# First attention pair of a clustered attention: its first head loaded to both halves of the partitions, its second head's clusters later

## The chip, the cores and the metric

One Trainium2 chip, one of its cores. The metric is the device time of one execution in microseconds. The core has TensorE (matmuls, PE in the rows), VectorE (DVE), ScalarE (ACT), GpSimd (POOL) and SyncE (SP, whose queue issues most transfers). Each engine runs its own list of instructions in order and waits on the others by semaphores.

## What is computed

Queries and keys of 16 pairs of batch and head are assigned to one of 16 clusters each, by the largest product with the normalized centroids; attention is taken inside a cluster only. Two MLPs follow.

```python
q_assign = np.argmax(np.einsum('bhsd,hcd->bhsc', q_n, c_n), axis=-1)
k_assign = np.argmax(np.einsum('bhsd,hcd->bhsc', k_n, c_n), axis=-1)
mask = q_assign[:, :, :, None] == k_assign[:, :, None, :]
scores = np.where(mask, scale * np.matmul(q, k.transpose(0, 1, 3, 2)), -1e9)
attn = softmax(scores)          # B=2, H=8, S=768, D=64
x = attn @ v                    # then x -> silu MLP -> gated MLP, 1536 tokens
```

All of it is float32 in quality: an operand is split in a rounded high part and a low part, and both go through the matmul.

## The kernel before

Heads go in pairs, p = 0 to 7, one head on partitions 0 to 63 (`L`) and one on 64 to 127 (`U`). A pair has 12 tiles of 128 queries, (p, j, i) with j the head and i = 0 to 5; "tile 0 to 5" below are those of the first head of pair 0. For each tile `scores` (L463) makes four matmuls into a PSUM buffer `s` of which there are two: two from `qa`, `ka`, in which the high part of a head stands on one half of the partitions and the low part of the query on the other, and two from `qm`, `km` (called `q` and `k` in the rows), which hold the high query, the low key and 16 rows each for the cluster masks. VectorE takes the negative maximum `nm`, ScalarE the exponential `e`, TensorE transposes `e` into `u` and `t` (two and four transposes), which VectorE and ScalarE copy into `ring` (called `ph`), and `values` (L511) multiplies with `vv`. A tile's `s` can be written again when the exponential two tiles before is done.

Clusters: `product_of_clusters` (L152) multiplies queries and keys with the centroids `cc` into `pm`, `scaled` (L276) brings them into `sums` (tile `sim`) on ScalarE, `similarities` (L165) transposes them into `ps`, and `ranked` (L170) finds on VectorE the maximum `mx`, the equal ones `eq`, their ranks `wq` and the first of them `mw`; two operations then write the choice `oh`. `choice_rows` transposes `oh` into `pt`, and `query_rows` and `key_rows` write the mask rows.

Pair 0 is written by hand ahead of the loop (L186 to L370). TensorE first runs `warm(n)`, products of zeros. The loads `qq`, `kk` bring both heads, one on each half; ScalarE makes the high parts `qh`, `kh` and VectorE the low part `ql`; nine transfers from buffer to buffer on SP's queue put them into `qa`, `ka` and `qm` of both heads. One `product_of_clusters` serves both heads. The first head is ranked from `ps` (`first_choice(0, ...)`), the second later from `sums` (`first_choice(1, ...)` in `first_masks`, L341). `zeros` clears operands and `oh` on GpSimd; `mine` on GpSimd copies `mw`, and only behind it the second head's clearing and its low key `late` are issued.

What sets the order: up to the end of `first` (L618) the instructions of TensorE, VectorE, ScalarE and SP stand as written; behind it only TensorE's do, and a scheduler places those of the other engines. In the loop `one_tile` (L648) runs the score of the tile two ahead, pieces of the next pair's preparation (`PIECES`, L643; the second head's masks are among the first of them), and the transposes of the tile.

## Time and profile before

| what | us |
|---|---|
| median of 3 runs | 773.4 |
| lowest, highest | 773.12, 774.94 |
| the profiled execution | 772.8 |
| its span, first to last instruction | 771.0 |
| TensorE busy in it | 761.3 (99%) |
| VectorE, ScalarE, GpSimd busy | 621.0, 403.5, 391.8 |

Rows give times from the start of the span. Busy times of matmuls overlap, and their ends are modelled; what matters is when one starts, what it waited for, and who waits for it.

### The profile page before, as it was taken

How to read it: one execution, taken by the hardware profiler on the slowest of the kernel's cores; microseconds unless marked ns; L12 is line 12 of the kernel's file. 1: busy time of each engine (PE TensorE's matmuls, PEld its weight loads, DVE VectorE, ACT ScalarE, POOL GpSimd, SP SyncE). 2: the span in 40 equal slices, each digit the busy share in tenths (PEclk: the TensorE clock that was granted, in tenths of full speed). 3: DMA queues.
4: the chain of work that ended last, by engine and by line, in shares of the span. 5: the costliest groups of instructions: out<-in, count | busy, mean ns of one | idle time of the engine just before them, and what ended most of it. 6: DMA issues, size and time to landing. Idle time of an engine off the chain costs nothing.

```text
span 771.0 us, 11463 instructions
## 1 busy us (share of the span) xinstructions
PE 761.3 (99%) x4314; PEld 652.6 (85%) x4314; DVE 621.0 (81%) x787; ACT 403.5 (52%) x691; POOL 391.8 (51%) x345
## 2 busy tenths in 40 slices
...
GB/s 222 159 203 194 114 146 195 122 123 201 32 76 79 57 83 83 55 110 82 88 78 82 54 55 58 88 75 56 34 76 55 82 83 55 55 82 55 1 0 164
DMA packets 25488, 71.61 MB, mean 93 GB/s; under 512 B 4484, under 2 KB 4952, under 8 KB 25432
## 3 DMA queue, kind: packets, MB, share of 16 engines
...
q8 instruction: 34, 0.56, 0.3%
...
HBM read 48.01 MB, written 3.19 MB: 66 GB/s over the span
## 4 chain that ended last, share of the span: by engine, by line
PE 92%; DVE 3%; ACT 2%; DMA 1%; issue 1%; POOL 0%; SPq 0%; ACTq 0%
PE z L1018 13%; PE s L468 8%; PE v L515 8%; PE t L507 5%; PE y L959 4%; PE h_0w L843 4%; PE h_0x L843 4%; PE g_0w L843 3%; PE g_0x L843 3%; PE v_0w L843 3%; PE v_0x L843 3%; PE u L496 3%; PE r L909 2%; PE q L909 2%; PE y_00None L959 2%; PE y_20None L959 2%
## 5 line engine op out<-in xcount | busy, mean ns | idle before, releaser
L476 DVE TENSOR_REDUCE nm<-s 128x1 f32<-128x768 f32 x96 | 91.5, 954 | 11.2 <-PE s L468 10.1
L481 ACT ACTIVATE e<-s,nm 128x768 f32<-128x768 f32 x96 | 86.5, 901 | 26.4 <-DVE nm L476 25.9
L1018 PE MATMUL z<-wu,ghb 128*128 128x512 f32 (+1 forms) x292 | 89.5, 388 | 0.0
L515 PE MATMUL v<-ph,vv 128*64 128x384 f32 x384 | 69.0, 494 | 0.2 <-DVE xf L527 0.2
L1018 PEld LDWEIGHTS z<-wu,ghb 128*128 128x128 f32 x292 | 54.2, 188 | 11.6 <-ACT ghb L64 0.5
L468 PE MATMUL s<-ka,qa 128*128 128x384 f32 x192 | 57.7, 381 | 2.0 <-ACT e L481 1.7
L507 PE MATMUL t<-ident,e 128*128 128x128 f32 x384 | 58.5, 275 | 0.8 <-ACT ph L64 0.3
L1018 PE MATMUL z<-wu,glb 128*128 128x512 f32 (+1 forms) x146 | 56.9, 390 | 0.0
L515 PEld LDWEIGHTS v<-ph,vv 128*64 128x64 f32 x384 | 24.7, 136 | 32.9 <-issue 29.0
L64 ACT ACTIVATE ph<-t 128x512 f32<-128x512 f32 x68 | 40.8, 600 | 21.4 <-PE t L507 20.5
L468 PE MATMUL s<-k,q 128*128 128x384 f32 x192 | 49.7, 339 | 0.0
L939 DVE TENSOR_TENSOR acc<-z,acc 128x1024 f32<-128x1024 f32 (+2 forms) x32 | 36.7, 1154 | 13.9 <-PE z L1018 13.2
L507 PEld LDWEIGHTS t<-ident,e 128*128 128x128 f32 x384 | 44.0, 140 | 4.2 <-DVE ph L67 3.2
L67 DVE COPY ph<-u 128x512 f32<-128x512 f32 x48 | 32.8, 683 | 16.3 <-PE u L496 16.3
L546 POOL TENSOR_TENSOR acc<-xf,rb 128x768 f32<-128x768 f32 x7 | 12.8, 1835 | 58.9 <-DVE nm L476 25.5
L496 PEld LDWEIGHTS u<-ident,e 128*128 128x128 f32 x192 | 23.3, 141 | 22.3 <-issue 18.6
L738 POOL TENSOR_TENSOR wo<-co,wo 128x512 fp32r<-128x512 f32 x16 | 22.0, 1383 | 35.5 <-ACT wo L64 35.5
L496 PE MATMUL u<-ident,e 128*128 128x128 f32 x192 | 38.6, 282 | 0.5 <-ACT e L481 0.5
L468 PEld LDWEIGHTS s<-k,q 128*128 128x128 f32 x192 | 34.5, 188 | 0.5 <-ACT k L338 0.3
L468 PEld LDWEIGHTS s<-ka,qa 128*128 128x128 f32 x192 | 28.9, 190 | 5.3 <-ACT e L481 3.4
L1018 PEld LDWEIGHTS z<-wu,glb 128*128 128x128 f32 x146 | 27.4, 188 | 7.0 <-DVE glb L899 1.4
L959 PE MATMUL y<-gha,wo 128*128 128x384 f32 x128 | 32.8, 334 | 0.0
...
## 6 DMA issues: line engine op xcount, KB each, us to landing
...
```

Source lines behind the costliest of these rows:

```text
L64: return nc.scalar.activation(o, i, AF.Copy)
L67: return nc.vector.tensor_copy(o, i)
L468: nc.tensor.matmul(s[:, g, 0:HS], lhsT=a[:, j, i * P : (i + 1) * P], rhs=c[:, j, g * HS : (g + 1) * HS], start=n == 0, stop=n == 1,)
L476: maxima.append(nc.vector.tensor_reduce(nm, s[:, :, 0:HS], axis=AX.XY, op=ALU.max, negate=True))
L481: x = nc.scalar.activation(e, s[:, :, 0:HS], AF.Exp, bias=nm, scale=1.0, accum_out=tots[p][:, n : n + 1])
L496: nc.tensor.transpose(both[:, kt - 4, i % 2, :], e[:, kt * P : (kt + 1) * P], ident)
L507: nc.tensor.transpose(t[:, kt, :], e[:, kt * P : (kt + 1) * P], ident)
L515: m = nc.tensor.matmul(o[(L, U)[kt % 2]], lhsT=vv[:, j, kt, :], rhs=ring[:, kt, g * G : (g + 1) * G], start=n < 2, stop=n >= NT - 2,)
L843: nc.tensor.matmul(o[:, b, 0:HS], lhsT=w[a][s][:, k, :], rhs=right[b, q][t][:, k, :], start=start and k == 0 and n == 0, stop=k == KQ - 1 ...
L939: added.append(nc.vector.tensor_tensor(z, o, z, op=ALU.add))
L959: nc.tensor.matmul(o[:, d, 0:width], lhsT=s[:, d, k, :], rhs=t[:, c], start=k == 0 and m == 0, stop=k == 1 and m == 2,)
L1018: nc.tensor.matmul(o[:, a, c], lhsT=s[:, q * P : (q + 1) * P], rhs=r[:, c], start=k == 0 and m == 0, stop=k == 1 and m == 2, skip_group_ch ...
```

## The change

In pair 0 the first head's queries and keys come from a new input `heads0` ([64, 2, 768]), loaded twice, onto rows 0 to 63 and onto rows 64 to 127 of the first two rows of `ring`, which is otherwise used only from the first transposed tile on. Its operands are cast from there straight into `ka`, `qa`, `qm`, `km`, and the low query is subtracted in place, so no transfer between buffers is left for it. `qq` and `kk` are loaded for the second head alone (rows 64 to 127); GpSimd splits it, and five transfers place it. The centroids arrive as one tile `ct` on all partitions and are copied by VectorE into the two places in `cc`.

The clusters' products become two calls: the first head's from rows 0 to 63 of the staged operands, at the old place; the second head's from rows 64 to 127 of `qq`, `kk`, behind the transposes of the first head's choice. Its scaling, transposes (`ps0_1`, behind tile 1's scores) and the cast into `sums` follow later too. `mine` goes; the second head's clearing stands ahead. The warming products are 7, 1, 4, 5 instead of 10, 1, 8, 5. Which engine copies which half of the first head's key rows is exchanged.

```diff
-WARM = (10, 1, 8, 5)
+WARM = (7, 1, 4, 5)
...
-        def product_of_clusters(pm, p, q, k):
+        def product_of_clusters(pm, p, q, k, rows=slice(0, P)):
...
-                        lhsT=cc[:, p % HP].rearrange("p j c -> p (j c)"),
-                        rhs=t.rearrange("p (i h c) -> p h i c", h=2, c=P)[:, h],
+                        lhsT=cc[rows, p % HP].rearrange("p j c -> p (j c)"),
+                        rhs=t[rows].rearrange("p (i h c) -> p h i c", h=2, c=P)[:, h],
...
-        for j, r in enumerate((L, U)):
-            act_dma(cc[r, :, j], cenT[j])
+        ct = cp.tile([P, HP, C], F32, tag="ct", name="ct")
+        act_dma(ct, cenT)
+        ring = wk.tile([P, NT, S], F32, tag="ph", name="ph", bufs=1)
+        staged = ring[:, 0], ring[:, 1]
+        for r in (L, U):
+            dma(ring[r, 0:2], heads0)
...
-        dma(qq, qT[0, 0])
-        dma(kk, kT[0, 0])
+        for t, a in zip((qq, kk), (qT, kT)):
+            dma(t[U], a[0, 0][U])
...
             zeros(0, 0)
+            zeros(0, 1)
...
+        for j, r in enumerate((L, U)):
+            nc.vector.tensor_copy(cc[r, :, j], ct[r])
...
-        nc.scalar.activation(qh, qq, AF.Copy, scale=scale)
-        nc.vector.scalar_tensor_tensor(ql, qq, scale, qh, op0=ALU.mult, op1=ALU.subtract)
-        cast(nc.scalar, kh, kk)
-        nc.vector.tensor_tensor(km[L, 0], kk[L], kh[L], op=ALU.subtract)
-
-        for j, (r, o) in enumerate(((L, U), (U, L))):
-            dma(qa[r, j].bitcast(F32), qh[r].bitcast(F32))
-            dma(ka[L, j].bitcast(F32), kh[r].bitcast(F32))
-            dma(ka[U, j].bitcast(F32), kh[r].bitcast(F32))
-            dma(qa[o, j].bitcast(F32), ql[r].bitcast(F32))
-            if j:
-                dma(qm[r, j].bitcast(F32), qh[r].bitcast(F32))
-        dma(vv, v[0, 0])
-
+        sq0, sk0 = staged
+        cast(nc.scalar, ka[L, 0], sk0[L])
+        nc.gpsimd.tensor_scalar(qm[L, 0], sq0[L], scale, 1.0, op0=ALU.mult, op1=ALU.mult)
         pm = ps_s.tile([P, 512], F32, tag="s", name="pm0")
-        product_of_clusters(pm, 0, qq, kk)
+        product_of_clusters(pm, 0, sq0, sk0, L)
         warm(WARM[1])
+        nc.vector.tensor_tensor(km[L, 0], sk0[L], ka[L, 0].bitcast(F32), op=ALU.subtract)
...
         scaled(0, sums, pm[:, 0:HS])
-        nc.scalar.activation(qm[L, 0], qq[L], AF.Copy, scale=scale)
...
         similarities(ps, sums)
+        nc.scalar.activation(qa[:, 0], sq0, AF.Copy, scale=scale)
+        cast(nc.scalar, ka[U, 0], sk0[U])
+        cast(nc.gpsimd, kh[U], kk[U])
+        nc.gpsimd.tensor_scalar(qh[U], qq[U], scale, 1.0, op0=ALU.mult, op1=ALU.mult)
         warm(WARM[2])
+        ex = sm.tile([P, 1], F32, tag="ex", name="ex", bufs=1)
+        nc.scalar.activation(ex, unit[:, 0:1], AF.Exp)
...
         for _ in first_choice(0, ps[:, 0:HS]):
             pass
-        cast(nc.scalar, sums, ps[:, 0:HS])
-        ex = sm.tile([P, 1], F32, tag="ex", name="ex", bufs=1)
-        nc.scalar.activation(ex, unit[:, 0:1], AF.Exp)
-        mine = sm.tile([P, 2 * NT], F32, tag="mine", name="mine", bufs=1)
-        with tc.issue_after(cast(nc.gpsimd, mine, chosen.pop()).ins):
-            with tc.issue_after(zeros(0, 1).ins):
-                late = nc.gpsimd.tensor_tensor(km[U, 1], kk[U], kh[U], op=ALU.subtract)
+        lows = nc.vector.scalar_tensor_tensor(
+            qa[U, 0], sq0[U], scale, qa[U, 0].bitcast(F32), op0=ALU.mult, op1=ALU.subtract
+        )
+        dma(qa[U, 1].bitcast(F32), qh[U].bitcast(F32))
+        dma(ka[L, 1].bitcast(F32), kh[U].bitcast(F32))
+        dma(ka[U, 1].bitcast(F32), kh[U].bitcast(F32))
+        dma(qm[U, 1].bitcast(F32), qh[U].bitcast(F32))
...
                 choice_rows(pts[n], 0, n * half + i, i)
+        pm = ps_s.tile([P, 512], F32, tag="s", name="pm0_1")
+        product_of_clusters(pm, 0, qq, kk, U)
+        with tc.issue_after(lows.ins):
+            nc.gpsimd.tensor_scalar(qq[U], qq[U], scale, 1.0, op0=ALU.mult, op1=ALU.mult)
+        lows = nc.gpsimd.tensor_tensor(ql[U], qq[U], qh[U], op=ALU.subtract)
+        dma(qa[L, 1].bitcast(F32), ql[U].bitcast(F32))
+        dma(vv, v[0, 0])
+        with tc.issue_after(lows.ins):
+            late = nc.gpsimd.tensor_tensor(km[U, 1], kk[U], kh[U], op=ALU.subtract)
         query_rows(0, pts[1], half, 0, 1)
-        chosen.append(key_rows(nc.vector, 0, pts[0], 0, 0, half))
-        key_rows(nc.scalar, 0, pts[1], 0, half, half)
+        key_rows(nc.scalar, 0, pts[0], 0, 0, half)
+        chosen.append(key_rows(nc.vector, 0, pts[1], 0, half, half))
         query_rows(0, pts[0], 1, 1, half - 1)
+        scaled(0, sums, pm[:, 0:HS])
         query_rows(0, pts[1], 0, half, half)
...
         for t in tiles[:2]:
             scores(*t)
+        ps = ps_t.tile([P, 512], F32, tag="t", name="ps0_1")
+        similarities(ps, sums)
+        cast(nc.scalar, sums, ps[:, 0:HS])
         warm(WARM[3])
```

Where instructions stand now. On VectorE, behind the maxima of tiles 0 and 1, before (the names end in buffer numbers; `nm_0_2` is the maximum of tile 2, and `mx_1` to `oh` with `mw_1` are the second head's ranking):

```order
L173 TENSOR_REDUCE mx_1_314<-sim_219 128x12
L176 TENSOR_TENSOR eq_1_316<-sim_219,mx_1_314 128x192
L178 TENSOR_TENSOR wq_1_318<-eq_1_316,rank 128x192
L476 TENSOR_REDUCE nm_0_2_310<-s_0_2_305 128x1
L181 TENSOR_REDUCE mw_1_356<-wq_1_318 128x12
L317 TENSOR_TENSOR oh_142<-wq_1_318,mw_1_356 128x6x16
L476 TENSOR_REDUCE nm_0_3_334<-s_0_3_329 128x1
L317 TENSOR_TENSOR oh_142<-wq_1_318,mw_1_356 128x6x16
L67 COPY ph<-u_0_0_320 128x2x256
L67 COPY ph<-t_0_1_341 128x4x128
L476 TENSOR_REDUCE nm_0_4_352<-s_0_4_347 128x1
```

On VectorE from tile 2's maximum on, after the change:

```order
L486 TENSOR_REDUCE nm_0_2_316<-s_0_2_311 128x1
L173 TENSOR_REDUCE mx_1_320<-sim_212 128x12
L176 TENSOR_TENSOR eq_1_322<-sim_212,mx_1_320 128x192
L486 TENSOR_REDUCE nm_0_3_340<-s_0_3_335 128x1
L67 COPY ph<-u_0_0_326 128x2x256
L178 TENSOR_TENSOR wq_1_324<-eq_1_322,rank 128x192
L67 COPY ph<-t_0_1_347 128x4x128
L486 TENSOR_REDUCE nm_0_4_358<-s_0_4_353 128x1
L181 TENSOR_REDUCE mw_1_362<-wq_1_324 128x12
L317 TENSOR_TENSOR oh_142<-wq_1_324,mw_1_362 128x6x16 x2
L339 CAST k_0_140<-pt_1_366 16x768
```

The second head's `mx` and `eq` have moved from ahead of tile 2's maximum to behind it, `wq` behind tile 3's, and `mw` and both writes of `oh` from around tile 3's maximum to behind tile 4's.

On TensorE, at the last transposes of the first head's choice and the first scores, before:

```order
L325 MATMUL pt_01_253<-identb,oh_142 64x128
L468 MATMUL s_0_0_273<-ka_195,qa_194 128x384 x2
L468 MATMUL s_0_0_273<-k_0_140,q_0_138 128x384 x2
L468 MATMUL s_0_1_283<-ka_195,qa_194 128x384 x2
L468 MATMUL s_0_1_283<-k_0_140,q_0_138 128x384 x2
```

On TensorE at the same place, after the change:

```order
L325 MATMUL pt_01_244<-identb,oh_142 64x128
L157 MATMUL pm_1_252<-qq_114,cc 32x384
L157 MATMUL pm_1_252<-kk_115,cc 32x384
L157 MATMUL pm_1_252<-qq_114,cc 32x384
L157 MATMUL pm_1_252<-kk_115,cc 32x384
L478 MATMUL s_0_0_274<-ka_199,qa_198 128x384 x2
L478 MATMUL s_0_0_274<-k_0_140,q_0_138 128x384 x2
L478 MATMUL s_0_1_284<-ka_199,qa_198 128x384 x2
L478 MATMUL s_0_1_284<-k_0_140,q_0_138 128x384 x2
L168 MATMUL ps_1_293<-ident,sim_212 128x128 x3
```

The second head's four cluster products now stand between the transposes and tile 0, and three transposes of its sums behind tile 1. The transposes of the second head's choice stay where they were, behind tile 4.

On ScalarE, from tile 3's exponential to the first of the second head (`e_1_0`), before (`pm_412`, `ps_436` and the `sim_411` written from them are pair 1's clusters):

```order
L481 ACTIVATE e_0_3_336,tot_281<-s_0_3_329,nm_0_3_334 128x768
L328 ACTIVATE q_0_138<-pt_1_360 16x384
L64 ACTIVATE ph<-t_0_2_382 128x4x128
L481 ACTIVATE e_0_4_354,tot_281<-s_0_4_347,nm_0_4_352 128x768
L328 ACTIVATE q_0_138<-pt_1_360 16x384
L277 ACTIVATE sim_411<-pm_412,unit 128x384
L481 ACTIVATE e_0_5_395,tot_281<-s_0_5_388,nm_0_5_393 128x768
L64 ACTIVATE sim_411<-ps_436 128x384
L64 ACTIVATE ph<-t_0_4_444 128x4x128
L481 ACTIVATE e_1_0_434,tot_281<-s_1_0_427,nm_1_0_432 128x768
```

On ScalarE in the same stretch, after the change:

```order
L491 ACTIVATE e_0_3_342,tot_282<-s_0_3_335,nm_0_3_340 128x768
L491 ACTIVATE e_0_4_360,tot_282<-s_0_4_353,nm_0_4_358 128x768
L328 ACTIVATE q_0_138<-pt_1_366 16x384
L64 ACTIVATE ph<-t_0_2_388 128x4x128
L328 ACTIVATE q_0_138<-pt_1_366 16x384
L491 ACTIVATE e_0_5_401,tot_282<-s_0_5_394,nm_0_5_399 128x768
L284 ACTIVATE sim_417<-pm_418,unit 128x384
L64 ACTIVATE sim_417<-ps_442 128x384
L491 ACTIVATE e_1_0_440,tot_282<-s_1_0_433,nm_1_0_438 128x768
L64 ACTIVATE ph<-t_0_4_450 128x4x128
```

The exponentials of tiles 4 and 5 now stand one step earlier, tile 5's ahead of the scaling of pair 1's `sim`.

## Rows read from the trace of the kernel before

**Rows 1.** Page of the profile, part 4: shares of the chain, by engine.

```profile
PE 92%; DVE 3%; ACT 2%; DMA 1%; issue 1%; POOL 0%; SPq 0%; ACTq 0%
```

**Rows 2.** Chain that ended last, from 0 to 60: start us, us, what.

```profile
7.59 3.34 DMA qa<-ql
...
18.41 0.45 PE pt L325 x6
...
20.48 0.85 PE pm L157 x8
...
22.98 0.33 PE ps L168 x3
...
30.76 0.96 PE s L468 x4
```

**Rows 3.** Timeline of TensorE: start us, us, engine line op out<-in xcount [idle before <-releaser].

```profile
1.32 4.36 PE L210 MATMUL pw<-wt 128*128 128x512 bf16 x10 [1.32 <-DVE sq L228]
5.78 0.48 PE L157 MATMUL pm<-qq,cc 128*32 128x384 f32 x1
...
6.10 0.48 PE L157 MATMUL pm<-qq,cc 128*32 128x384 f32 x1
...
7.80 1.89 PE L210 MATMUL pw<-wt 128*128 128x512 bf16 x8
10.13 0.55 PE L325 MATMUL pt<-identb,oh 128*64 128x128 bf16 x7 [0.45 <-DVE oh L317]
10.97 0.62 PE L468 MATMUL s<-ka,qa 128*128 128x384 f32 x2 [0.29 <-DMA qa<-ql]
...
14.24 0.62 PE L468 MATMUL s<-ka,qa 128*128 128x384 f32 x2 [0.28 <-ACT e L481]
...
17.43 0.62 PE L468 MATMUL s<-ka,qa 128*128 128x384 f32 x2 [0.22 <-ACT e L481]
```

**Rows 4.** Timeline of VectorE, same columns, 9 to 19 us.

```profile
9.07 0.35 DVE L181 TENSOR_REDUCE mw<-wq 128x12 bf16<-128x192 bf16 x1
9.53 0.46 DVE L317 TENSOR_TENSOR oh<-wq,mw 128x96 bf16<-128x96 bf16 x2
...
12.20 1.82 DVE L476 TENSOR_REDUCE nm<-s 128x1 f32<-128x768 f32 x2 [1.09 <-PE s L468]
13.94 0.34 DVE L173 TENSOR_REDUCE mx<-sim 128x12 f32<-128x192 f32 x1
...
14.71 0.26 DVE L178 TENSOR_TENSOR wq<-eq,rank 128x192 bf16<-128x192 bf16 x1
15.24 0.96 DVE L476 TENSOR_REDUCE nm<-s 128x1 f32<-128x768 f32 x1 [0.28 <-PE s L468]
16.12 0.34 DVE L181 TENSOR_REDUCE mw<-wq 128x12 bf16<-128x192 bf16 x1
...
18.30 0.68 DVE L67 COPY ph<-t 128x512 f32<-128x512 f32 x1
18.93 0.96 DVE L476 TENSOR_REDUCE nm<-s 128x1 f32<-128x768 f32 x1
```

**Rows 5.** Timeline of ScalarE, same columns.

```profile
4.34 0.84 ACT L284 ACTIVATE qh<-qq 128x768 fp32r<-128x768 f32 x1 [0.21 <-DMA qq<-in_qT]
...
6.72 0.58 ACT L277 ACTIVATE sim<-pm,unit 128x384 f32<-128x384 f32 x1 [0.39 <-PE pm L157]
...
21.48 0.56 ACT L277 ACTIVATE sim<-pm,unit 128x384 f32<-128x384 f32 x1
21.95 0.90 ACT L481 ACTIVATE e<-s,nm 128x768 f32<-128x768 f32 x1
```

**Rows 6.** Stretches: us, busy by engine, PEclk, DMA share, GB/s.

```profile
3.25:3.50 0.25, 0.25 (x2) 0.07 (x1) 0.22 (x2) 0.25 (x1) 0.25 (x1) 1.00 1.07 420
...
6.75:7.00 0.25, 0.20 (x1) 0.00 (x0) 0.25 (x1) 0.25 (x1) 0.00 (x0) 1.00 1.02 221
```

**Rows 7.** Timeline of GpSimd, columns as in the other timelines.

```profile
9.52 0.20 POOL L66 TENSOR_SCALAR mine<-mw 128x12 f32<-128x12 bf16 x1 [5.92 <-DVE mw L181]
```

10 lines of the change are left out of this document (4 added, 6 removed).

## The prediction

> **What bounds the kernel now.** I read the shares of the chain first: TensorE carries 92% of it [rows 1], so a microsecond is gained or lost only where TensorE waits, and the change touches the first 31 us. The profiled execution took 772.8 us. Next the merged chain of that stretch [rows 2]: the first score product waits for the copy of `ql`, which lands at 7.59 + 3.34 = 10.93; from 18.41 TensorE works almost in one row, and up to the product at 30.76 it hands over to the other engines and back without slack. A shift of TensorE at 18.41 therefore should go through to the end; I found no load behind it that anything waits for. Beyond the first tiles of the second head the listings of all engines are alike in both kernels, so every difference has to come from this stretch.
>
> Then TensorE by itself [rows 3]. The clusters' product `pm` starts at 5.78, the transposes of the choice (`pt`) at 10.13, score tile 0 at 10.97, tile 2 at 14.24, tile 4 at 17.43. Ten warming products take 4.36 us, 0.44 each; eight later ones 1.89, 0.24 each. So TensorE stands at its 1.2 GHz level until 5.68, and at 2.4 GHz from the cluster products on, whose second round follows 0.32 behind the first. The granted clock is given as 1.00 in the early stretches too [rows 6]; I go by the spacing. Last VectorE [rows 4]: behind the maxima of tiles 0 and 1 it ranks the second head (`mx` at 13.94, then `eq`, `wq` at 14.71) in the gap before tile 2's maximum at 15.24, so the choice `oh` is there when TensorE comes to transpose it right behind tile 4.
>
> **The front: a lead of 0.3 us.** Only the first head must land before `pm`. Seven warming products end at 1.32 + 7 × 0.44 = 4.4, which is the floor. The load is as large as that of `qq`, for which ScalarE waited until 4.34 [rows 5]; but it goes to 64 partitions. 64-row copies moved 221 GB/s, the 128-row loads 420 [rows 6]. The copy also reads SBUF, the load HBM, so 4.34 is one end; the other has 393 KB at 221 instead of 420 GB/s, 1.78 for 0.94 us, thus 5.2. I take 4.75, about the middle.
>
> The Trainium skill, page "SBUF — State Buffer", section "Door 1: The DMA port swizzle (why [64,N] ≈ [32,N])", states that partitions 0 to 63 reach only half of the DMA ports; that speaks against staging each half by itself. The trace agrees for copies, 221 against 420 GB/s [rows 6]. By the page the load would land at the late end, 5.2, and the lead below would be 0.45 smaller.
>
> Products from 64 rows run as long as from 128, since the columns are as many; but `pm` at 4.75 falls where TensorE was still at 1.2 GHz before. Two rounds of 0.32 would cost 0.65 more in full, nothing if the clock rises earlier; I take 0.4. From `pm` to its scaling `sim` it was 6.72 − 5.78 = 0.94 [rows 3, 5], so `sim` starts at 4.75 + 0.94 + 0.4 = 6.1 instead of 6.72, a lead of 0.62. The casts into `ka`, `qa` and `km` fit beside this. Reduction, choice and transposes keep their durations: `pt` at 10.13 − 0.62 = 9.5. New behind it stands `pm` of the second head: 0.52 for seven transposes (six take 0.45) and 0.85 for the products [rows 2], so tile 0 starts at 10.9. The low part of `qa`, on VectorE right behind the choice, is as wide as a maximum (0.9) and done at 10.3, the mask rows behind it in time for tile 0's mask products. Before, tile 0 lost 0.23 on such a row: its maximum stood 1.23 behind its start, tile 2's only 1.00 [rows 3, 4]. So the first maximum comes at 11.9 instead of 12.20: lead 0.3. Tile 2 waits for the first exponential, 14.24 − 12.20 = 2.04 behind that maximum, thus 13.94; five warming products and three new transposes end at about the same time. With both bounds (4.4 and full clock, 5.2 and half) the lead goes from 1.1 to −0.4.
>
> Nine copies between buffers that become five, the zeroing moved ahead and five new GpSimd operations I cost at nothing: GpSimd had an idle 5.9 us before `mine` [rows 7], which take the early ones; the late ones (scaling, `ql`, `km`) delay the zeroing for pair 1 and with it pair 1's split by about 1 us, whose first reader is the product for pair 1 at 20.48 [rows 2], itself later now. Without that cover it would be that 1 us.
>
> **The middle: 2.8 us lost.** The second head is now ranked from `sums` that exist only after tile 1, and VectorE's listing puts `mw` and both `oh` behind tile 4's maximum. TensorE's listing still has the transposes right behind tile 4, and behind those everything else. Counted from tile 2's start S with the spacings of [rows 4]: its maximum at S + 1.00; `mx` 0.88 later; `mx` and `eq` take 0.77, so tile 3's maximum stands at S + 2.65; the copy of `u` 0.88 later; `wq` 0.63; the copy of `t` 0.26; tile 4's maximum 0.63, S + 5.05; `mw` 0.88; `oh` 0.46 later; both `oh` 0.46; the transposes 0.14 behind (9.99 to 10.13). That is S + 7.0. Before it was 18.41 − 14.24 = 4.17. Tile 4 is issued by S + 4.2, so TensorE stands 2.8 us, and nothing covers it: **+2.82**. Between ends: were VectorE not behind, tile 4's maximum would start at S + 4.2 (its products 1.0 behind 17.43 − 14.24 = 3.19) and the loss be 2.0; with 0.1 more at each of the four dependent steps it is 3.2. ScalarE's cast of `sums` fits into its wait for the first `t`.
>
> **A second, small wait.** ScalarE now takes tile 5's exponential ahead of pair 1's `sim`; before, `sim` at 21.48 stood ahead of the exponential at 21.95 [rows 5]. Behind the transposes at 18.41, tile 5's maximum comes after 2.3, its exponential 1.0 later, `sim` 0.9, and its reader on TensorE 0.7 after that: 4.9, where TensorE wants it after 22.98 − 18.41 = 4.57 [rows 2]. **+0.33**, between 0 and 0.5.
>
> **Sum.** −0.30 + 2.82 + 0.33 = +2.85: 775.6 us for the profiled execution. Its 772.8 lies 0.6 below the median of the runs, 773.4, so on that footing 776.2.
>
> **Rivals.**
>
> *The whole lead and little else* (not slower). The first load lands by 4.4 and the cluster products run at 2.4 GHz; the lead is 1.1 and ScalarE's swap costs 0.1: −1.1 + 2.8 + 0.1 = +1.8, 775.2. It decides at `sim`: before 5.5, this is the case. For it: the cluster rows arrive in a quarter of the pieces and share the engines less. Against it: only seven warming products ran before, and 221 GB/s.
>
> *TensorE falls to 1.2 GHz in the hole.* The 2.8 us are longer than any wait of TensorE before. Its row from 18.41 to 22.98 would go at half rate for some part, 0 to 4.6 more; with half of it, 2.3: 778.5. For it: the early warming shows that the level follows what ran. Against it: no row of before shows a fall. The Trainium skill, page "TensorE: Matmul & The Clock Gate", section "HAM oscillation — how this bites in real kernels", says that waiting between bursts can return the array to half rate; no run here shows it.
>
> *The loads come late.* Both halves at half rate and queued: `pm` at 5.8 as before, `pt` at 10.13, tile 0 at 11.5, first maximum 12.5. The −0.3 turns into +0.3: sum +3.45, 776.8. It decides if the first half lands after 5.4.
>
> *VectorE is not behind.* The loss is 2.0, with the lead of 0.3 and the small wait +2.0: 775.4.
>
> **How the numbers follow.** A change under 0.3% (2.3 us) is about what a measurement of this kernel can't tell from none. Forecast 0.45 (776.2, its own range 775.5 to 776.9); whole lead 0.17; VectorE not behind 0.12; late loads 0.10; clock falls 0.12; a gain that I don't see 0.04. Slower by over 0.3%, above 775.7: three quarters of the forecast, the late loads, the clock, 0.02 of the rest: 0.34 + 0.10 + 0.12 + 0.02 = 0.58. Same 0.38, faster 0.04. The range goes from a little below the whole lead to the clock case: 774.6 to 778.5.
>
> **What would show it.** In the profile after: `pm` between 4.4 and 5.2 with its rounds over 0.4 apart; `sim` near 6.1; tile 0 near 10.9, tile 2 near 13.9; then TensorE waits 2 to 3 us before the transposes of the second head's choice, which `oh` on VectorE ends, near 20.9 instead of 18.41; and products behind the hole spaced as before. Wrong would be: no such wait; a lead over 1.5; or a shift at 31 us that the end doesn't have.

## Result: 778.8 us, and the profile after

The changed kernel takes 778.78 us (median of 4 runs, 778.46 to 779.63), the kernel before 773.29 on the same chip (773.12 to 774.94): a ratio of 1.0071, 95% interval 1.0057 to 1.0085. It is slower, as forecast, but by 5.5 us where 2.85 were worked out, and 0.3 above the range. The profiled execution took 778.46 us with a span of 776.7, against 772.8 and 771.0.

TensorE's share of the chain falls, VectorE's rises; before it was [rows 1]:

```profile
PE 90%; DVE 5%; ACT 2%; DMA 1%; issue 1%; POOL 0%; SPq 0%; ACTq 0%; POOLq 0%; DVEq 0%
```

TensorE after, against [rows 3]; start us, us, engine line op out<-in xcount [idle before <-releaser]:

```profile
5.73 0.85 PE L157 MATMUL pm<-ph,cc 64*32 64x384 f32 x8 [1.24 <-DVE r L278]
...
7.75 0.58 PE L168 MATMUL ps<-ident,sim 128*128 128x128 f32 x3 [0.85 <-ACT sim L284]
...
10.52 0.92 PE L325 MATMUL pt<-identb,oh 128*64 128x128 bf16 x7 [0.48 <-DVE oh L317]
...
12.19 0.61 PE L478 MATMUL s<-ka,qa 128*128 128x384 f32 x2
...
15.39 0.69 PE L478 MATMUL s<-ka,qa 128*128 128x384 f32 x2
...
18.72 0.61 PE L478 MATMUL s<-ka,qa 128*128 128x384 f32 x2 [0.28 <-ACT e L491]
...
22.08 0.85 PE L325 MATMUL pt<-identb,oh 128*64 128x128 bf16 x6 [2.39 <-DVE oh L317]
```

The products `pm` start when they did before, 5.73 against 5.78, although only half of the rows is needed; tile 0 is 1.22 late, tile 2 1.15, tile 4 1.29. Then TensorE waits 2.39 us for `oh`; the transposes that stood at 18.41 [rows 2] now stand at 22.08.

VectorE after, against [rows 4], and its centroid work at the front:

```profile
3.83 1.21 DVE L273 COPY cc<-ct 64x64 f32<-64x64 f32 x2
...
5.69 0.83 DVE L279 TENSOR_TENSOR r<-r,r 128x4 f32<-128x4 f32 x1
...
6.75 0.18 DVE L281 RECIPROCAL unit<-r 128x4 f32<-128x4 f32 x1
...
17.46 0.35 DVE L173 TENSOR_REDUCE mx<-sim 128x12 f32<-128x192 f32 x1
...
19.59 0.25 DVE L178 TENSOR_TENSOR wq<-eq,rank 128x192 bf16<-128x192 bf16 x1
...
20.36 0.95 DVE L486 TENSOR_REDUCE nm<-s 128x1 f32<-128x768 f32 x1
21.22 0.34 DVE L181 TENSOR_REDUCE mw<-wq 128x12 bf16<-128x192 bf16 x1
21.59 0.43 DVE L317 TENSOR_TENSOR oh<-wq,mw 128x96 bf16<-128x96 bf16 x2
```

The order is the one foreseen: `mx` behind tile 2's maximum, `mw` and `oh` behind tile 4's. New is the front: two small copies take 1.21 us, an addition of 4 columns 0.83, so `unit` comes at 6.75 (5.18 in the trace of before). ScalarE after, against [rows 5]:

```profile
5.62 0.84 ACT L64 ACTIVATE ka<-ph 64x768 fp32r<-64x768 f32 x1 [1.47 <-DMA ph<-in_heads]
7.03 0.58 ACT L284 ACTIVATE sim<-pm,unit 128x384 f32<-128x384 f32 x1 [0.56 <-DVE unit L281]
...
26.58 0.90 ACT L491 ACTIVATE e<-s,nm 128x768 f32<-128x768 f32 x1 [1.19 <-DVE nm L486]
...
27.48 0.57 ACT L284 ACTIVATE sim<-pm,unit 128x384 f32<-128x384 f32 x1
```

The first cast waits until 5.62 for the rows, and `sim` 0.56 for `unit`. At 26.58 stands the exponential that now precedes pair 1's `sim`. Stretches, against [rows 6]; us, busy by engine, PEclk (granted clock), DMA share, GB/s:

```profile
9.00:10.00 1.00, 1.00 (x3) 0.13 (x1) 0.83 (x4) 0.98 (x2) 1.00 (x2) 0.50 0.00 0
...
22.00:23.00 1.00, 0.92 (x7) 0.75 (x8) 0.02 (x1) 0.43 (x3) 0.90 (x2) 0.50 0.08 33
...
25.00:26.00 1.00, 1.00 (x11) 0.33 (x9) 0.47 (x1) 0.39 (x2) 1.00 (x2) 0.92 1.03 224
```

Twice the granted clock is 0.50, that is 1.2 GHz: from 8.1 to 11.5 us, and from 21.7 to 25.2, in and behind the wait of 2.39. In before it is 1.00 through the first 36 us.

So the loss can be followed by TensorE's delay against before: 1.15 at tile 2, 3.67 at the second head's transposes (22.08 against 18.41), 4.80 at the first tile behind pair 1's products (26.84 against 22.04), 5.34 at the next (29.06 against 23.72). In the rows of VectorE it stays at 5.34 to 5.45 (once 5.65) to the end of attention at 240 us; the MLPs add 0.3.

### The profile page after: what moved, and what is told of

It reads as the page before. It is cut to its first block, busy times and chain, and to the rows that moved or that the text cites. A ratio compares the mean times of both kernels' runs of the same rounds, so it can differ in the third digit from the quotient of the medians.

```text
span 776.7 us, 11472 instructions
## 1 busy us (share of the span) xinstructions
PE 763.1 (98%) x4317; PEld 654.0 (84%) x4318; DVE 623.0 (80%) x789; ACT 404.0 (52%) x692; POOL 397.1 (51%) x349
## 4 chain that ended last, share of the span: by engine, by line
PE 90%; DVE 5%; ACT 2%; DMA 1%; issue 1%; POOL 0%; SPq 0%; ACTq 0%; POOLq 0%; DVEq 0%
PE z L1030 13%; PE v L524 7%; PE s L478 7%; PE y L971 4%; PE t L516 4%; PE h_0w L855 4%; PE h_0x L855 4%; PE g_0w L855 3%; PE g_0x L855 3%; PE v_0w L855 3%; PE v_0x L855 3%; PE u L505 2%; PE r L921 2%; PE q L921 2%; PE y_00None L971 2%; PE y_20None L971 2%
## 5 line engine op out<-in xcount | busy, mean ns | idle before, releaser
L951 DVE TENSOR_TENSOR acc<-z,acc 128x1024 f32<-128x1024 f32 (+2 forms) x32 | 36.7, 1153 | 13.7 <-PE z L1030 13.1
```

Source lines behind the costliest of these rows:

```text
L951: added.append(nc.vector.tensor_tensor(z, o, z, op=ALU.add))
```

## Experiments

Each is written as an edit of the kernel after, if nothing else is said. Times are medians, with the lowest and highest run, the ratio to before on the same chip and its 95% interval. A run's *clock* is its mean granted clock: 3.5 us at 0.50 take 0.002 off it. Tiles (0,1,0) and (0,1,1) are the first two of the second head of pair 0. The *delay* is how much later than before the first `xf` row of VectorE (27.82 us before, 33.17 after) starts in the profile.

### Theories at the start

A: the hole in TensorE's row, its wait for a choice that is made too late, is the cause; with it a fall of the clock. B: the front is, that is the loads and TensorE's clock there. The first four kernels fill the hole with products, restore the old warming, move the choice further back, and put the late products alone into the kernel before.

**e1_warm_hole**

```diff
+            warm(11)
             for i in range(NT):
                 choice_rows(pt, 1, i, i)
```

> The changed kernel with eleven warming products put between tile 4's scores and the transposes of the second head's choice; eleven at 0.22 us fill the wait of 2.4 us there and nothing else moves. Theory A (the wait costs twice: once as a wait, and once more because TensorE goes on at 1.2 GHz behind it for 3 us): the transposes stay near 22.1, but take 0.45 instead of 0.85, and pair 1's cluster product comes 1.2 to 1.3 us earlier than 25.42; time 778.8 - 1.3 = 777.5. Theory B (the wait alone costs, the slower products behind it lie beside VectorE's and ScalarE's work): the spacing goes back to 2.4 GHz, but tile (0,1,0) stays near 26.8 and the time at 778.8.

Measured 783.26 us (781.68 to 784.49), 1.0126 [1.0111, 1.0141]; neither theory.

**e3_choice_later**

```diff
-            (2, 0, 2, 1, 1, 4, 0, 0, 1, 0, 0, 0),
+            (2, 0, 0, 3, 1, 4, 0, 0, 1, 0, 0, 0),
```

> The changed kernel with one number pair of the table of pieces altered: the transposes of the second head's choice stand behind tile 5's scores instead of tile 4's, so two transposes sets and tile 5's scores (1.5 us) run in the wait. Theory A (the order of the choice makes the wait): the wait shrinks from 2.4 to about 1 us, TensorE keeps 2.4 GHz behind it, tile (0,1,0) comes 2 to 2.7 us earlier than 26.84, time 776.1 to 776.8. Theory B (VectorE's chain from tile 2 to the second head's mask rows is the bound, wherever the transposes stand): the wait only moves behind tile 5, tile (0,1,0) gains less than 0.5, time 778.3 to 778.8.

Measured 783.93 (780.89 to 785.48), 1.0131 [1.0103, 1.0159]; neither.

**e4_late_alone** (the kernel before, with the second head's products, scaling and similarities at after's places)

```diff
-        product_of_clusters(pm, 0, qq, kk)
+        product_of_clusters(pm, 0, qq, kk, L)
...
+        pm = ps_s.tile([P, 512], F32, tag="s", name="pm0_1")
+        product_of_clusters(pm, 0, qq, kk, U)
...
+        ps = ps_t.tile([P, 512], F32, tag="t", name="ps0_1")
+        similarities(ps, sums)
+        cast(nc.scalar, sums, ps[:, 0:HS])
```

> The kernel before with one part of the change alone: first head's cluster product from rows 0 to 63, the second head's behind the transposes of the first choice, its scaling, transposes and cast as in the changed kernel; loads, copies, zeroing and warming stay as before. Theory A (the later second head is the loss, the new loading costs 1 us beside it): tile 0 some 0.5 later than 10.97, a wait of 2.4 us behind tile 4, half clock behind it (1.3), ScalarE's swap 0.4; time 773.3 + 4.5 = 777.8. Theory B (the loss lies in the new loads and casts): 773.3 + 1 = 774.3 or less.

Measured 781.08 (779.63 to 782.04), 1.0097 [1.0082, 1.0112]: the order alone costs about as much as the whole change (1.0071, and 1.0098 when it was measured again, e18). All three traces show what neither theory had. VectorE in e4_late_alone, then GpSimd in the same stretch:

```profile
21.36 0.33 DVE L181 TENSOR_REDUCE mw<-wq 128x12 bf16<-128x192 bf16 x1
21.73 2.19 DVE L317 TENSOR_TENSOR oh<-wq,mw 128x96 bf16<-128x96 bf16 x2
```

```profile
22.01 1.80 POOL L402 TENSOR_TENSOR kl<-kk,kh 128x768 fp32r<-128x768 f32 x1
```

Two comparisons that take 0.43 us in after take 2.19 here (2.67 in e3, 3.53 in e1), while GpSimd subtracts for pair 1. The later the choice, the surer it meets that work; after's own choice ends at 22.0, just as GpSimd's next casts begin. In e1 and e3 TensorE's front was slow too (below).

**e2_warm_front**

```diff
-WARM = (7, 1, 4, 5)
+WARM = (10, 1, 9, 5)
```

> The changed kernel with ten warming products at the start instead of seven, and nine instead of four behind the first transposes. Both sets end before what follows is ready (5.7 and 10.4 us), so they delay nothing. Theory A (TensorE dropped to 1.2 GHz at 8 us because it had been idle since 4.5 us but for the cluster product): granted clock 1.00 from 8 to 12, transposes of the first choice 0.55 instead of 0.92, second cluster product 0.85 instead of 1.2, tile 0 at 11.6 instead of 12.2, time 778.2. Theory B (the front is set by the late load and by VectorE, the clock lies beside it): tile 0 stays at 12.2, time 778.8.

Measured 778.26 (777.25 to 780.10), 1.0065 [1.0049, 1.0081]: as both theories allow. Its trace has `pt` at 10.73 in full rate, yet tile 4 at 18.57, against 18.72: the clock at the front costs little when it falls as late as in after.

### Does GpSimd stop VectorE?

**e7_split_held** (e4, with an edge)

```diff
+            with tc.issue_after(split_behind[0].ins):
                 on_pool["split", p] = nc.gpsimd.tensor_tensor(kl, kk, kh, op=ALU.subtract)
```

> The kernel of e4 (before, with the second head's products of clusters alone put behind the transposes), with pair 1's two 128x768 subtractions on GpSimd held until the second head's last comparison on VectorE is done. Theory A (while GpSimd subtracts with two tensor operands, VectorE's bf16 comparison stands still, 2.19 us for two instead of 0.43 to 0.46): the two comparisons take 0.45 us, the second head's choice is transposed 1.7 us sooner, at 22.3, and the kernel takes 779.3 us (778.5 to 780). Theory B (the comparisons are slow for another cause, or the hole costs by the clock of TensorE alone): comparisons 2 us again, and 781.1.

Measured 780.32 (778.97 to 781.24), 1.0087 [1.0069, 1.0105]. The edge held nothing: GpSimd's subtraction starts before the second comparison ends. But the trace is the clearest there is. The two comparisons one by one, then GpSimd:

```profile
L318 DVE TENSOR_TENSOR oh<-wq,mw x2: 776/1316/1855, 21.2 to 21.9; 128x96 bf16<-128x96 bf16 x2
```

```profile
21.07 0.83 POOL L66 TENSOR_SCALAR qh<-qq 128x768 fp32r<-128x768 f32 x1
21.86 1.80 POOL L406 TENSOR_TENSOR kl<-kk,kh 128x768 fp32r<-128x768 f32 x1
```

The first starts at 21.23 and takes 0.78: it ends at 22.0, 0.1 behind GpSimd's cast. The second takes 1.86 and ends at 23.78, 0.1 behind GpSimd's subtraction.

**e9_really_held** (e4, with GpSimd made to read the last comparison first)

```diff
+                seen = sm.tile([P, NT], F32, tag="seen", name="seen", bufs=1)
+                copied_choice = cast(nc.gpsimd, seen, oh[0][:, :, 1, 1, 0])
+                behind_choice = lambda: tc.issue_after(copied_choice.ins)
+            with behind_choice():
+                cast(nc.gpsimd, qh, qq)
```

> The kernel of e4 (before, with the second head's products alone behind the transposes), with a copy of six numbers a row of the second head's last comparison put into GpSimd's queue ahead of pair 1's two casts and two subtractions, so that none of the four starts before that comparison is done (the edge of e7 ordered nothing across engines: there the first comparison took 0.78 us and ended 0.1 us after a cast of GpSimd, the second 1.86 us and ended 0.1 us after a subtraction). Theory A (a VectorE write of this kind waits for the end of the instruction that GpSimd runs): both comparisons take 0.43 to 0.46 us together, the transposes of the second head's choice start at 22.2 instead of 23.8 to 24.0, and the kernel takes 779.3 us (778.5 to 780) against 781.1 and 780.3 of e4 and e7. Theory B (the comparisons are slow for VectorE's or the bank's own reasons): 2 us again, 781 us or, with pair 1's operands later as well, 782.

Measured 779.39 (778.42 to 780.42), 1.0083 [1.0068, 1.0098], where 779.3 was expected. The comparisons:

```profile
L317 DVE TENSOR_TENSOR oh<-wq,mw x2: 252/255/258, 20.7 to 20.8; 128x96 bf16<-128x96 bf16 x2
```

0.25 us each. The wait ahead of the transposes is 2.31 us instead of 4.76, the delay 4.02 instead of 7.24 (5.2 against 8.0 by 77 us, for a cause not followed up). So the blocking is real, and it is part of why e1, e3 and e4 came out above both theories. In e1 and e3 the slow front is another part: it puts tile 4 at 22.70 and 22.38 instead of 18.72. The times alone, whose intervals overlap with e4's and e7's, would not show the blocking, and what still lies between e9 and the 777.8 that A gave for e4 was not taken apart.

### The front

**e5_zeros_later**

```diff
             zeros(0, 0)
-            zeros(0, 1)
...
+        with tc.issue_after(nc.gpsimd.tensor_scalar(qm[L, 0], sq0[L], scale, 1.0, op0=ALU.mult, op1=ALU.mult).ins):
+            zeros(0, 1)
```

> After, with GpSimd's two 64x768 fills for the second head issued behind its scaled copy of the first head's q instead of ahead of it. Theory A (GpSimd's work from 3.5 to 6.5 us holds up VectorE's copies of the centroids, 1.21 us for two, and its additions, 0.83 us instead of 0.16, so that unit comes at 6.75 and the first similarity copy on ScalarE at 7.03 waits for it by 0.56): the centroid copies take some 0.5 us for the two, unit comes by 6.2, the similarity copy at 6.6 behind the product of clusters, and the kernel gains 0.4: 778.4 us. Theory B (the front is late by the loads and TensorE's clock, unit has slack): within 0.2 of after, 778.8. Either way under 1 us.

Measured 780.51 (777.45 to 783.22), 1.0094 [1.0057, 1.0131]. The first half of A holds: the copies of the centroids take 0.40 us for two, and `unit` comes at 5.24. But TensorE's rows and a stretch of the same trace:

```profile
5.96 1.51 PE L157 MATMUL pm<-ph,cc 64*32 64x384 f32 x8 [1.47 <-DMA ph<-in_heads]
...
11.56 0.93 PE L325 MATMUL pt<-identb,oh 128*64 128x128 bf16 x7 [0.73 <-DVE oh L317]
...
13.86 1.01 PE L478 MATMUL s<-ka,qa 128*128 128x384 f32 x2
```

```profile
12.00:14.00 2.00, 2.00 (x14) 0.59 (x12) 0.96 (x2) 1.11 (x3) 0.00 (x0) 1.00 0.96 207
```

Products and transposes go at half rate from 5.96 to 16 us (1.51 for `pm` instead of 0.85, 0.93 for `pt` instead of 0.55), while PEclk says 1.00; the column does not tell that TensorE never rose. The profiles of e1, e3 and e12 have the same front. All four run seven warming products, which end at 4.49, and then wait for the rows.

This profile shows two things more. TensorE waits for the second head's choice as long as in after, 2.39 us, and goes on at full rate (0.52 for the transposes, 0.85 in after; PEclk is 1.00 through 40 us):

```profile
24.37 0.52 PE L325 MATMUL pt<-identb,oh 128*64 128x128 bf16 x6 [2.39 <-DVE oh L317]
```

Tile (0,1,0) follows at 27.89, 3.52 behind, where after takes 4.76 (26.84 − 22.08). So a wait of this length did not always bring a fall of the clock, and the fall costs 1.24 us up to that tile. And ScalarE has after's order, the exponential ahead of pair 1's `sim`:

```profile
27.60 0.90 ACT L491 ACTIVATE e<-s,nm 128x768 f32<-128x768 f32 x1 [0.57 <-DVE nm L486]
28.49 0.57 ACT L283 ACTIVATE sim<-pm,unit 128x384 f32<-128x384 f32 x1
```

TensorE waits 0.28 us for this `sim`, and its delay goes from 5.85 at tile (0,1,0) to 6.35 at the next (30.07 against 23.72): the order costs 0.50 at full rate.

**e6_one_load** (`heads0` laid out twice in memory, so 128 rows)

```diff
-        for r in (L, U):
-            dma(ring[r, 0:2], heads0)
+        dma(ring[:, 0:2], heads0)
```

> After, with the first head's q and k laid out twice in memory, so that one transfer of 128 rows fills both halves instead of two transfers of 64 rows. Theory A (the two transfers of half the partitions are what lands late, ScalarE starting at 5.6 instead of 4.3): the first cast starts at 4.8, the first product of clusters at 5.0, tile 0 at 11.4, and the kernel takes 778.0. Theory B (the bytes are what lands late: 786 KB in both forms, while the loads of before first brought q, then k): cast at 5.6 again, 778.8. Theory C (a row of DRAM read twice was cheaper than two rows): later than 5.6, 779.3.

Measured 784.42 (783.45 to 785.97), 1.0143 [1.0126, 1.0160]: the first cast starts at 6.53, later than after's 5.62, as only C allows, and the time is 5.1 us above C's. The delay, 7.19, is the front's, a hole of 3.04 (comparisons 1.08 beside GpSimd's cast) and half rate from 22.2 to 28.9 us. Whether the second head's rows beside it are what makes it late was not tried apart.

**e18_after_again** (no edit)

> After, unchanged, once more beside the others. Theory A (with 7 and 4 warming products TensorE falls to half rate at 8.2 us in some executions and at 5.9 in others, as in the profiles of e6 and e8 and of e1, e3, e5 and e12): the times spread by 2 us or more, 777.3 to 783 us, while before's stay within 1. Theory B (the four kernels with the early fall owe it to their edits): within 1.2 us of 778.8, as in the first four runs.

Measured 779.77, the runs 779.77, 783.57, 779.75, 779.68, 783.47, 779.78; 1.0098 [1.0081, 1.0115]. A: the changed kernel has executions 4 us apart, before's eleven lie within 1. The first four runs did not show the longer ones. The profile is of the run of 779.77: `pm` takes 0.85 as in after, and the granted clock is 0.50 from 7.6 to 11.0 us and from 21.2 to 28.1, the second time twice as long as in after; tile (0,1,1) is 6.09 late. The runs of 783.47 and 783.57 us have clock 0.989, those of 779.75 and 779.78 have 1.000; none of them has a profile, so that the two kinds of front of A set them apart is not shown.

### Undoing the order, undoing the clock

**e8_choice_early**

```diff
+        product_of_clusters(pm, 0, qq, kk, U)
+        scaled(0, sums, pm[:, 0:HS])
         choice_rows(pts[1], 0, 0, half)
...
+        similarities(ps, sums)
+        cast(nc.scalar, sums, ps[:, 0:HS])
         query_rows(0, pts[1], half, 0, 1)
```

> After, with its loads and casts, but with the second head's products of clusters ahead of the first head's transposes (as before), and its similarities ahead of the first tile. Theory A (of the 5.5 us that the change costs, the late choice takes 2.4 in its wait and 1.3 in TensorE's clock behind it, the front 1.3 and ScalarE's order 0.3): the wait ahead of the second head's transposes is under 0.4 us, no half clock follows it, and the kernel takes 775.1 us (774.5 to 776.2, since the product waits for the second head's rows, which land by 9.2). Theory B (the front's lateness is the larger share, and the wait only moves): 777.5 or more. Theory C (the products wait so long for the second head's rows that the first head's transposes, at 10.7, fall behind by 1 us): 776.5.

Measured 778.25 (777.51 to 779.39), 1.0063 [1.0048, 1.0078]: no hole, as A says, and no gain, as B says. ScalarE's copy stood ahead of the mask rows, so tile 0's second half waited 0.88, and the granted clock is 0.50 from 8.2 to 18.5: the few warming products do not keep TensorE at full rate.

**e10_early_warm** (e8, the copy behind the mask rows, and the old warming)

```diff
-WARM = (7, 1, 4, 5)
+WARM = (10, 1, 8, 5)
...
         query_rows(0, pts[1], 0, half, half)
+        cast(nc.scalar, sums, ps[:, 0:HS])
```

> After's loads and casts, with the second head's products ahead of the first head's transposes, ScalarE's copy of its similarities behind the first head's mask rows (in e8 it stood ahead of them, and tile 0's second half waited 0.88 us), and 10 and 8 warming products as before instead of 7 and 4. Theory A (e8 lost its gain to half clock from 8.6 to 19 us and to that order): granted clock 1.0 through the first 30 us, tile 0 at 11.5, tile 4 at 18.2, no wait over 0.4 us ahead of the second head's transposes; 774.9 us (774.2 to 776). Theory B (the new loads cost by what they take from ScalarE and VectorE as well): 777 or more with the clock at 1.0.

Measured 774.05 (773.82 to 774.85, 10 runs), 1.0016 [1.0006, 1.0025], below A. TensorE:

```profile
11.03 0.58 PE L325 MATMUL pt<-identb,oh 128*64 128x128 bf16 x7
...
12.19 0.59 PE L481 MATMUL s<-ka,qa 128*128 128x384 f32 x2
...
18.68 0.62 PE L481 MATMUL s<-ka,qa 128*128 128x384 f32 x2 [0.27 <-ACT e L494]
...
19.58 0.52 PE L325 MATMUL pt<-identb,oh 128*64 128x128 bf16 x6
```

No wait ahead of the transposes at 19.58, full rate from 7.3 us on, delay 1.21, and 1.06 at the end of attention. Against e2, which differs in the place of the second head's work alone but for one warming product, the order is worth 3.9 us: e2 lies 4.9 above before on its chip, e10 1.1. The 1.1 remain with the new loads and casts.

**e12_held_warm** (after with e9's hold and e1's products)

> After, with pair 1's casts and subtractions on GpSimd held behind the second head's last comparison as in e9, and with e1's eleven warming products ahead of the second head's transposes. Theory A (the clock falls to 0.50 behind the hole because TensorE stands still in it, and e1 lost its gain since the later choice met GpSimd's subtractions): comparisons 0.43 us, granted clock 1.0 over 22 to 25 us, pair 1's products 3.4 us behind the second head's transposes or less (3.34 in after at half clock, 2.1 at full clock); 777.5 us (776.8 to 778.5). Theory B (the warming products themselves hold the transposes up by as much as they save): 778.8, as after. Theory C (holding pair 1's split makes its operands late): 779 or more with the clock at 1.0.

Measured 779.14 (777.47 to 779.77), 1.0076 [1.0061, 1.0091]. The comparisons take 0.42, and from the second head's transposes to tile (0,1,0) it is 3.52 instead of 4.76, as A says; but its profile has the half-rate front of e5 (tile 0 at 13.84), so the gain was not to be seen in the time. Nor does it show that the products made the gain: e5, with the same front and without products or hold, has 3.52 too.

**e14_front_and_hole_warm** (e12 with e2's warming)

```diff
-WARM = (7, 1, 4, 5)
+WARM = (10, 1, 9, 5)
...
+            warm(11)
...
+                copied_choice = cast(nc.gpsimd, seen, oh[0][:, :, 1, 1, 0])
```

> After, with 10 and 9 warming products at the front as in e2, eleven ahead of the second head's transposes as in e12, and pair 1's split held behind the last comparison as in e9 and e12. Theory A (e12 gained 1.24 us in the stretch from the second head's transposes to tile (0,1,0), 3.52 us against 4.76 in after, and lost it to a front at half rate from 5.9 to 16 us that four fewer warming products allow): no product at half rate in the first 30 us, tile 4 at 18.6, the second head's transposes at 22.0, tile (0,1,0) 3.5 us later, 777.0 us (776.5 to 777.8). Theory B (the gain in the hole is given back later): 778.3, as e2. In both, what is left against before is the hole of 2.4 us, the front of 1.2 and ScalarE's order of 0.3.

Measured 777.20 (777.12 to 777.46), 1.0052 [1.0040, 1.0065]; A, row by row:

```profile
18.48 0.62 PE L486 MATMUL s<-ka,qa 128*128 128x384 f32 x2 [0.28 <-ACT e L499]
...
19.29 2.55 PE L214 MATMUL pw<-wt 128*128 128x512 bf16 x11
21.84 0.52 PE L325 MATMUL pt<-identb,oh 128*64 128x128 bf16 x6
...
25.36 0.60 PE L486 MATMUL s<-ka,qa 128*128 128x384 f32 x2
...
27.04 0.59 PE L486 MATMUL s<-ka,qa 128*128 128x384 f32 x2
```

```profile
22.00:24.00 2.00, 1.92 (x20) 1.54 (x22) 1.04 (x2) 1.33 (x5) 2.00 (x4) 1.00 0.00 0
```

The transposes still come at 21.84, 3.36 behind tile 4 as in after (22.08 − 18.72): the warming hides nothing, it only keeps the rate. Tile (0,1,0) follows at 25.36, 3.32 behind before, and the next at 27.04, 3.32 as well. In after these are 4.80 and 5.34, so e14 is 2.0 us ahead at the second. Of that, 0.24 stand ahead of the wait (tile 4), and 1.24 between the transposes and tile (0,1,0), 3.52 against 4.76, as in e5: this is the half rate behind the wait. The last 0.54 are not. In this kernel ScalarE has before's order again, pair 1's `sim` ahead of the exponential, and TensorE does not wait for it:

```profile
24.95 0.58 ACT L284 ACTIVATE sim<-pm,unit 128x384 f32<-128x384 f32 x1 [0.57 <-PE pm L157]
25.42 0.90 ACT L499 ACTIVATE e<-s,nm 128x768 f32<-128x768 f32 x1
```

e14's five runs lie within 0.4 us, with clock 0.999 or 1.000. Of e2's four, with the same warming at the front and nothing in the wait, one has 1.000 (777.25 us) and three have 0.996 to 0.998 (777.72 to 780.10). So with the products and the hold the clock did not fall in any run, and without them it fell in most.

**e15_between_tiles** (after's order; loads of e13, 10 and 8 warming products; similarities between tiles 0 and 1)

```diff
-        for t in tiles[:2]:
-            scores(*t)
+        scores(*tiles[0])
         ps = ps_t.tile([P, 512], F32, tag="t", name="ps0_1")
         similarities(ps, sums)
         cast(nc.scalar, sums, ps[:, 0:HS])
+        scores(*tiles[1])
```

> After's order of the second head's products (behind the first head's transposes) with the loads of e13, 10 and 8 warming products, and the second head's similarities between tile 0 and tile 1 on TensorE, their copy between the exponentials of the two on ScalarE (in after it stood behind both, and VectorE's first step of the choice came behind tile 2's maximum at 17.46). Theory A (the hole is only that the choice starts one tile's maximum too late on VectorE): its first step comes at 15.5 or before, ahead of tile 2's maximum, the wait ahead of the second head's transposes is 0 to 0.9 us, and the kernel takes 773.4 us (772.6 to 774.4). Theory B (VectorE has no room for the choice before tile 4 in any case, as the last two comparisons fall behind tile 3's copies): wait of 1.5 us or more and 775 to 777.

Measured 776.47 (776.05 to 780.52), 1.0045 [1.0031, 1.0058]: B. In the profile (its longest run) `mx` comes at 16.76, still behind tile 1's maximum and now ahead of tile 2's, but both comparisons still behind tile 3's copies, at 21.80, beside GpSimd's casts (1.56 us); the wait is 2.08. One place earlier was not enough there. That profile has the granted clock at 0.50 from 13.1 to 16.8 us, ahead of the choice; the three runs with clock 1.000, at 776.05 to 776.47 us, are B's too, but their rows are not known.

### What is left of the front

**e13_two_loads** (e10; q and k each laid out twice, as in before's loads)

```diff
-        for r in (L, U):
-            dma(ring[r, 0:2], heads0)
+        for n in range(2):
+            dma(ring[:, n], heads0[n])
...
         nc.vector.reciprocal(unit, r4)
+        for t, a in zip((qq, kk), (qT, kT)):
+            nc.vector.memset(t[U, 0:1], 0.0)
+            dma(t[U], a[0, 0][U])
```

> e10, with the first head's q and k, each laid out twice in memory, as two transfers of 128 rows of 3 KB (the form that before's two loads have) instead of two of 64 rows of 6 KB, and with the transfers of the second head's rows not issued before VectorE is done with unit (5.3 to 6.1 us). Theory A (what is left of the loss in e10, 1.1 us, is that the rows of the first head land at 5.8 instead of 4.3 and 5.5, and that the second head's products hold TensorE ahead of the first head's transposes): the first product of clusters runs at 5.6 to 5.7, tile 0 comes at 11.0 to 11.4, and the kernel takes 773.2 us (772.6 to 773.8). Theory B (the loss lies behind the loads, in the casts and GpSimd's fills): 774 as e10. Theory C (the second head's rows now land so late, after 9, that its products hold the first head's transposes up): 774.6 or more.

Measured 775.81 (775.22 to 775.90), 1.0032 [1.0021, 1.0044]: C. The first products start at 5.04, 0.9 before e10's, so the 384 KB of q in 128 rows land sooner than 384 KB in 64 rows, even alone (6.05 in e11, below). But the second head's products wait for their rows until 9.93 and hold the first head's transposes until 11.52: tile 0 at 12.66.

**e11_half_first** (e10 with e5's fills; the lower half loaded alone, the upper copied from it)

```diff
-        for r in (L, U):
-            dma(ring[r, 0:2], heads0)
+        dma(ring[L, 0:2], heads0)
+        dma(ring[U, 0:2], ring[L, 0:2])
```

> e10, with the first head's rows loaded once, into the lower half of the partitions, and copied from there to the upper half by a second transfer, and with the second head's fills behind GpSimd's cast of q as in e5. Theory A (the two transfers of 64 rows share the 0.2 to 0.37 MB/us that the front's rows show, so that the first half lands only with most of the second: 0.69 of 0.79 MB were moved by 5.4 us): the first half lands by 4.4, the first product runs at 4.5, unit is ready at 5.3, tile 0 comes at 10.4 to 11.0, and the kernel takes 773.6 us (772.5 to 774.6), level with before. Theory B (the first half lands no sooner, the transfers of 64 rows take the time of 128): 775, as e10. Theory C (the upper half now lands after 7.5 and the casts for tile 0 wait for it): 776.

Measured 776.08 (776.07 to 776.39), 1.0041 [1.0026, 1.0056]: B and C together. Stretches, and ScalarE's first cast:

```profile
3.75:4.00 0.25, 0.25 (x2) 0.15 (x1) 0.22 (x3) 0.09 (x1) 0.00 (x0) 1.00 0.89 369
4.25:4.50 0.25, 0.25 (x2) 0.15 (x1) 0.21 (x2) 0.00 (x0) 0.00 (x0) 1.00 0.43 98
4.50:4.75 0.25, 0.25 (x2) 0.04 (x1) 0.22 (x2) 0.00 (x0) 0.00 (x0) 1.00 0.30 74
4.75:5.00 0.25, 0.25 (x3) 0.11 (x1) 0.21 (x2) 0.00 (x0) 0.00 (x0) 1.00 0.02 0
```

```profile
5.93 0.84 ACT L64 ACTIVATE ka<-ph 64x768 fp32r<-64x768 f32 x1 [1.82 <-DMA ph<-in_heads]
```

The transfer's bytes are moved by 4.8 us, yet the cast starts at 5.93. Fewer rows in flight did not make the first half come sooner; the upper half lands at 9.68.

**e16_rows_sooner** (e13 with the second head's rows issued behind `csq`, and 4 warming products ahead of their products)

```diff
-WARM = (10, 1, 8, 5)
+WARM = (10, 1, 4, 5)
...
         nc.vector.tensor_tensor(csq, cr, cr, op=ALU.mult)
+        for t, a in zip((qq, kk), (qT, kT)):
+            nc.vector.memset(t[U, 0:1], 0.0)
+            dma(t[U], a[0, 0][U])
```

> e13, with the transfers of the second head's rows issued behind VectorE's squares of the centroids, at 3.5 and 4.1 us instead of 6.7 and 7.3, and with 4 warming products instead of 8 ahead of its products of clusters. Theory A (with q and k as two transfers of 128 rows and the second head's rows close behind, nothing is left of the loss but ScalarE's copy of the products ahead of the mask rows): the second head's products at 8.7, the first head's transposes at 9.9 to 10.1, tile 0 at 11.2 to 11.4, tile 4 at 17.8; 773.4 us (772.8 to 774.0), the same as before within what can be measured. Theory B (the later rows now take bandwidth from k again): first product ends after 6.6, tile 0 at 11.8 or later, 774 or more. Theory C (TensorE falls to half rate with four fewer warming products, as in e1, e3, e5 and e12): products of 0.84 us in the first 16 us, 775 or more.

Measured 779.85 (775.69 to 780.53), 1.0073 [1.0057, 1.0089]. The second head's products run at 8.81, as A says; then GpSimd's work for that head, now sooner too, stops VectorE on the first tile's path. VectorE, then GpSimd:

```profile
9.77 1.05 DVE L318 TENSOR_TENSOR oh<-wq,mw 128x96 bf16<-128x96 bf16 x2
10.85 2.57 DVE L354 SCALAR_TENSOR_TENSOR qa<-ph,qa 64x768 fp32r<-64x768 f32 x1
```

```profile
10.80 1.81 POOL L372 TENSOR_TENSOR ql<-qq,qh 64x768 fp32r<-64x768 f32 x1
```

The low part of q takes 2.57 us instead of 0.95, tile 0 starts at 13.48 behind it, and TensorE falls to half rate in that wait. No theory had this.

**e17_kept_apart** (e16, GpSimd made to read that low part first)

```diff
+        seen0 = sm.tile([P, NT], F32, tag="seen0", name="seen0", bufs=1)
+        with tc.issue_after(cast(nc.gpsimd, seen0[U], qa[U, 0, 0:NT].bitcast(F32)).ins):
             nc.gpsimd.tensor_scalar(qq[U], qq[U], scale, 1.0, op0=ALU.mult, op1=ALU.mult)
```

> e16, with a copy of six numbers a row of the first head's low part of q (VectorE's work) put into GpSimd's queue ahead of its scaling and its two subtractions for the second head, so that none of the three runs beside that low part. Theory A (in e16 the low part took 2.57 us instead of 0.95, from 10.85 on, because GpSimd's subtraction ran from 10.80 to 12.61, and the first comparisons 1.05 us instead of 0.43 beside GpSimd's scaling from 9.84; the fall to half rate at 13 is the wait of TensorE behind that): comparisons 0.43 us, low part 0.96, tile 0 at 11.2 to 11.6, no half rate in the first 24 us, 773.4 us (772.8 to 774.2), all runs within 1 us. Theory B (GpSimd is now so late, by some 1.5 us, that pair 1's split or the second head's operands wait): 775 or more with tile 0 at 11.4.

Measured 776.48 (776.10 to 776.84), 1.0040 [1.0027, 1.0053]. The low part takes 0.96, tile 0 starts at 11.29, 0.32 behind before; and GpSimd's next subtraction, of the low key (14.15 to 15.98), now meets the second head's `eq`:

```profile
14.79 1.41 DVE L176 TENSOR_TENSOR eq<-sim,mx 128x192 bf16<-128x192 f32 x1
```

1.41 us instead of 0.36, which puts tile 4 at 18.44. Delay 1.16, 1.55 at the end of attention; 1.9 more come behind 563 us, in the second MLP, where nothing was edited: ScalarE waits there for a load of weights (`ru`) until 564.14, 3.6 behind before. Why that load comes late stays open. No version beat the kernel before.

## Why the prediction fell short

**The front: +1.15 at tile 2, where −0.30 stood.** The step that failed is "I take 4.75, about the middle" for the first landing. It was 5.6 (5.62 to 5.88 in after, e8, e10 and e18), beyond the late end, 5.2, and past the 5.4 from which the rival of the late loads decides. The other loads beside it are not the cause: with nothing beside it the first half was read at 5.93 (e11). What puts it behind 5.2 stays open. That rival priced the lost lead at 0.6; it was 1.45, in three terms. From `pm` to `pt` the lost time is 1.02 (10.52 against 9.5): the load's 0.98, 0.36 for `unit` (7.03 against 5.73 + 0.94) and 0.08 behind it, less the 0.4 taken for half rate in `pm`, which did not occur. Half rate from 8.1 us on makes `pt` and the second `pm` 0.27 longer. Tile 2 is 0.16 late on the warming products, longer than foreseen. "GpSimd's new operations I cost at nothing" is part of it: the early fills lengthen VectorE's copies from 0.40 to 1.21 us (e5), and the cast of q its addition. The late end for the load was the one that the Trainium skill gave ("SBUF — State Buffer", section "Door 1: The DMA port swizzle (why [64,N] ≈ [32,N])"); the trace went past it in the same direction.

**The middle: right.** Foreseen was S + 7.0 for the transposes, found 22.08 − 15.39 = 6.69, and a loss of 2.52 (6.69 less 4.17) where 2.82 stood, between 2.0 and 3.2. The order on VectorE was read rightly; e10, which has the products early, has no wait.

**The fall to 1.2 GHz: named, priced, and given 0.12.** "With half of it, 2.3: 778.5" was the rival; the granted clock is 0.50 from 21.7 to 25.2 us, and against e5 and e14, which keep the rate, that costs 1.24 us between the transposes and tile (0,1,0) (4.76 against 3.52). In e18, where it lasts to 28.1 us, tile (0,1,1) comes 7.77 behind the transposes instead of 5.70 in e5: 2.1 us. It belonged into the sum: no wait of TensorE this long stood in before's trace, so the missing fall there spoke neither way, and of the eleven profiles here in which TensorE stands for 2.08 us or more ahead of these transposes, ten show it; e5's does not. What the Trainium skill says in "TensorE: Matmul & The Clock Gate", section "HAM oscillation — how this bites in real kernels", the trace now shows: 0.50 behind a wait of 2.39, 1.00 in e14.

**The second small wait: right, a little too small.** +0.33 was foreseen, between 0 and 0.5; 5.34 − 4.80 = +0.54 was found, and +0.50 in e5, where TensorE is at full rate and ScalarE has the same order. With before's order, in e14, it is 0. In e2 and e18, where half rate lasted longer, tile (0,1,0) itself comes 6.1 late and the next loses only 0.01 more.

**The sum.** 1.15 + 2.52 + 1.13 (4.80 − 3.67) + 0.54 = 5.34, against −0.30 + 2.82 + 0 + 0.33. The missing 2.5 us are 1.45 of the front and 1.13 of the clock; the other two terms nearly cancel. That the range's upper end, 778.5, comes so near is luck: it stands for the clock with 2.3 us and a front that leads by 0.3, where the clock took 1.1 and the front was late. "Wrong would be: a shift at 31 us that the end doesn't have" did not occur. What the time of the changed kernel is, is less sharp than the first four runs say: with e18 its ten runs go from 778.46 to 783.57.
